# Linear-memory attention with a gated feed-forward block: transposed memory keys for two batches, and softmax denominators on VectorE for six

## The chip, the cores and the metric

The kernel runs on one NeuronCore of a Trainium2 chip. A core has five engines with queues of their own: TensorE (PE in the profile, its weight loads PEld), VectorE (DVE), ScalarE (ACT), GpSimd (POOL) and SyncE (SP), which here only issues DMAs. The metric is the device time of one execution in microseconds (us). Times vary a little from run to run, so a kernel is given by the median of several executions. One more execution is recorded by the profiler, and every duration of a single instruction comes from that one.

## The reference

There are 8 batches with 8 heads, 576 positions (S), head width 64 (D) and 32 memory slots (M). Per batch and head:

```python
a = softmax(phi, axis=positions)           # S x 32: each memory slot's weights over the positions
k_m, v_m = a.T @ k, a.T @ v                # 32 x 64 each: the memory's keys and values
attn = softmax(q @ k_m.T / 8, axis=memory) # S x 32: each position's weights over the slots
x = attn @ v_m                             # S x 64
```

The heads of a position are put side by side to a row of 512, and a feed-forward block with a gate follows, for 4608 rows:

```python
out = (silu(x @ w_gate) * (x @ w_val)) @ w_out   # 512 -> 1536 -> 512
```

## The kernel before

**Layout of the memory work.** The load of phi, k and v puts a pair of heads on 128 partitions: 64 partitions for each head, nine positions on each. So a matmul over 64 partitions and nine accumulation steps sums over the positions of one head. The kernel never forms x. Since x = attn @ v_m, it multiplies the memory's values with the gate and value weights first (`u_round`, tiles U), and then U with the attention (`gv_half`): that is one step over 128 partitions per group of four heads, 2 groups (g) per batch. A group's 128 partitions are 4 heads x 32 slots.

**Memory keys and values.** `kv_denominators` sums the phi exponentials over the positions with matmuls against a column of ones, one sum S for each head and slot; `kv_reciprocal` makes their reciprocals rS. In batches 2 to 7, `kv_items` sums keys and values together, scales both by rS on VectorE (`k_norm`, `v_norm`) and turns them with TensorE's transposes (`kv_T`) into kT, a tile of three 128-column blocks: the keys of group 0 and of group 1, and the values. In batches 0 and 1 the exponentials lie in a masked layout (`phi_exp_masked`, with zeros in the other head's rows). There the keys go the way of `k_items`: denominators, sums, `k_norm`, `kv_T`. The values are made by `v_direct`, which takes v as the stationary operand and the masked exponentials as the moving one, so that the product comes out transposed; four VectorE copies (L349) put it into kT, unscaled, and U is scaled by rS when it is evacuated (L457, L461).

**Attention.** q is transposed on TensorE for batches 0 and 1 (`q_T`) and by a transposing DMA for the others (`load_qT`). `scores(b, g)` makes 8 matmuls of a group into two banks (r, halves of the positions) and ScalarE takes the exponentials E with the factor 1/8 (L394). `z_inv(b, g)` makes the denominators: two matmuls with `bones`, a matrix with ones in 32x32 blocks on its diagonal (L405), give each column's sum over a head's 32 slots on all its partitions; two logarithms (L408) and one exponential of the negative (L410) on ScalarE give the reciprocal lz. `norm(b, g)` multiplies E by lz on VectorE into A (L415).

**Feed-forward.** A batch has 24 slots. `gv_slot` makes a gate product (two matmuls of 288 columns), silu on ScalarE (L494), and, one slot later, the value product and the multiplication on VectorE into h (L501). The output projection (L538) runs in tiles of 128 rows with 12 units of one 512-column matmul each; a full tile is copied to SBUF on VectorE ("v", L550) or ScalarE ("a", L548) and stored from SP.

**What sets the order.** Every engine's order is the order of the calls, written out by hand (`manual_schedule`). PSUM's 8 banks come from a list, oldest release first (`bank`, `done`). From batch 2 on, each batch begins with output units of the batch before (`take(n)` issues n of them), among which the scores, the value-weight round `u_values`, denominators and normalisation are placed; then the 24 slots follow, with the rest of the output units, the next batch's memory work and its U spread among them (`spread`). `phi_sum` on GpSimd adds the next batch's exponentials and waits for a batch's A (L213). Before batch 2 there is no output work to put between the steps: `warm(n)` issues dummy matmuls there (n units of 128 columns). `exp_tables()` and `preload_act_table_set` switch ScalarE's function table.

**Loads.** Inputs are loaded by GpSimd in one queue in the order of the calls: keys and q of batches 0 and 1, their values, the weights of the gate and value projections (two half blocks of block 0 for each, then blocks 1 and 2, L141), then the output weights mixed with the inputs of batches 2 and 3.

Of the kernel before, what the change touches and what calls it, by code (L numbers as in the profile page):

```python
# [9 lines left out]
FP32 = mybir.dt.float32  # L10
BF16 = mybir.dt.bfloat16
# [3 lines left out]
def kernel(  # L15
# [19 lines left out]
    nc = tc.nc  # L35
# [4 lines left out]
    M = phi.shape[3]  # L40
# [4 lines left out]
    NP = H // 2  # L45
    NJF = DF // 128
    HALF = S // 2
    CH = 512
    NCH = DF // CH
    sm_scale = 1.0 / math.sqrt(D)  # L50
# [22 lines left out]
    def bank(shape, dtype, name):  # L73
        tag = free.pop(0)
        t = ps.tile(shape, dtype, tag=tag, name=name)
        held[id(t)] = tag, t
        return t

    def done(*tiles):

        for t in tiles:
            free.append(held.pop(id(t))[0])
# [142 lines left out]
    def kv_sum(b, p, parts):  # L225


        w0, w1 = parts[0], parts[-1] + 1
        n = (w1 - w0) * D
        for j in range(JK):  # L230
            for i in range(NP):
                for g in range(NG):
                    nc.tensor.matmul(  # L233
                        p[g][32 * i:32 * i + 32, 0:n],
                        lhsT=phi_of(b, g, j, i),
                        rhs=kvs[b][64 * g:64 * g + 64, w0:w1, i, j * D:(j + 1) * D],
                        start=(j == 0),
                        stop=(j == JK - 1),
                        tile_position=(64 * g, 32 * i),
                    )  # L240
# [71 lines left out]

        return [run_sums, lambda: kv_T(b, (0, 1))]

    def k_items(b):


        def denominators():
            p = bank([128, NG], FP32, "p_S")
            kv_denominators(b, p)  # L320
            kv_reciprocal(b, p)
            done(p)

        def sums():
            p = [bank([128, D], FP32, f"p_kv{g}") for g in range(NG)]
            kv_sum(b, p, (0,))
            k_norm(b, p)
            done(*p)

        return [denominators, sums, lambda: kv_T(b, (0,))]  # L330

    def v_direct(b):

        p = bank([128, NP // 2, NG, M], FP32, "p_vT")
        for n in range(NP // 2):
            for j in range(JK):
                for o in range(2):
                    nc.tensor.matmul(
                        p[64 * o:64 * o + 64, n],
                        lhsT=kvs[b][:, 1, 2 * n + o, j * D:(j + 1) * D],  # L340
                        rhs=masked[b][:, j, :, 2 * n + o],
                        start=(j == 0),
                        stop=(j == JK - 1),
                        tile_position=(0, 64 * o),
                    )
        dst = kTs[b][:, 2].rearrange("p (n o m) -> p n o m", n=NP // 2, o=2)
        for g in range(NG):
            for o in range(2):
                nc.vector.tensor_copy(  # L349
                    out=dst[64 * g:64 * g + 64, :, o], in_=p[64 * o:64 * o + 64, :, g]  # L350
                )
        done(p)
        scaled.add(b)

# [25 lines left out]
    def scores(b, g):  # L380
        p = gv_banks()
        for i in range(NP):
            for r in range(2):
                nc.tensor.matmul(  # L384
                    p[r][32 * i:32 * i + 32, 0:HALF],
                    lhsT=kTs[b][64 * r:64 * r + 64, g, 32 * i:32 * i + 32],
                    rhs=qTs[b, i][64 * r:64 * r + 64, g],
                    start=True,
                    stop=True,
                    tile_position=(64 * r, 32 * i),  # L390
                )
        e = att.tile([128, 2, HALF], BF16, tag=f"E{g}", name="t_E")
        for r in range(2):
            nc.scalar.activation(out=e[:, r], in_=p[r][:, 0:HALF], func=AF.Exp, scale=sm_scale)  # L394
        done(*p)
        es[b, g] = e

# [2 lines left out]
    def z_inv(b, g):  # L400

        p = gv_banks()
        lz = att.tile([128, 2, HALF], FP32, tag="lz", name="t_lz")
        for r in range(2):
            nc.tensor.matmul(  # L405
                p[r][:, 0:HALF], lhsT=bones, rhs=es[b, g][:, r], start=True, stop=True
            )
            nc.scalar.activation(out=lz[:, r], in_=p[r][:, 0:HALF], func=AF.Ln)  # L408
        done(*p)
        nc.scalar.activation(out=lz, in_=lz, func=AF.Exp, scale=-1.0)  # L410
        lzs[b, g] = lz

    def norm(b, g):
# [178 lines left out]
    def out_list(b):  # L592
        tiles = range(0, 4) if b % 2 == 0 else range(4, 9)
        res = []
        for n, u in enumerate(tiles):
            if b + 1 == B and u == tiles[-1]:
                res += out_units_end(b // 2, u)
            else:
                res += out_units(b // 2, u, "v" if n % 4 != 3 else "a")
        return res  # L600

    def q_items(b, evac):
# [15 lines left out]

    def u_values(b):

        u_round(b, (((1,), 1, (0, 1)),), "vv")
    def run(items):
        for x in items:
            x()
# [13 lines left out]
    def gv_slots(b):  # L638
        return [lambda s=s: gv_slot(b, s) for s in range(2 * NJF)]

    def warm(n):


        p = bank([128, DM], FP32, "p_warm")
        x = bones.rearrange("p (a c) -> p a c", a=1)
        sizes = [4] * (n // 4)
        sizes += [n - sum(sizes)] if n > sum(sizes) else []
        for a in sizes:
            nc.tensor.matmul(  # L649
                p[:, 0:128 * a],  # L650
                lhsT=bones,
                rhs=x.to_broadcast([128, a, 128]) if a > 1 else bones,
                start=True,
                stop=True,
            )
        free.insert(0, held.pop(id(p))[0])
# [40 lines left out]


    warm(104)
    k0, k1 = k_items(0), k_items(1)  # L700
    q0, q1 = q_items(0, "vvvv"), q_items(1, "vvvv")
    run(k0[:2])
    warm(8)
    run(k0[2:] + k1[:1])
    warm(10)
    run(q0[:2])
    warm(3)
    scores(0, 0)
    run(q0[2:])
    warm(2)  # L710
    z_inv(0, 0)
    scores(0, 1)
    warm(3)
    run(k1[1:2])
    z_inv(0, 1)
    warm(2)
    run(k1[2:] + q1[:2])
    warm(4)
    scores(1, 0)
    norm(0, 0)  # L720
    run(q1[2:])
    norm(0, 1)
    warm(2)
    scores(1, 1)
    z_inv(1, 0)
    z_inv(1, 1)
    v_direct(0)
    nc.scalar.preload_act_table_set("silu_and_others")
    norm(1, 0)
    norm(1, 1)  # L730
    warm(24)
    v_direct(1)
    warm(4)


    g0, g1 = gv_slots(0), gv_slots(1)
    run([u_half(0, (0,), 0, 0, "av"), u_half(1, (0,), 0, 0, "av")])
    warm(6)
    for s in range(4):
        gv_gate(0, s)  # L740
    run([u_half(0, (1,), 0, 0, "va"), u_half(1, (1,), 0, 0, "va")])
# [20 lines left out]
    for b in range(2, B):  # L762
        last = b + 1 == B
        exp_tables()
        if b == 2:
            load_qT(2)
            phi_exp(2)
            run(take(28))
            run(kv_items(2)[:1] + take(6) + kv_items(2)[1:] + take(14))
        run(take(4))  # L770
        u_values(b)
        for g in range(NG):
            scores(b, g)
        if b == 2:
            load_k(3)
            load_v(3)
            load_q(4)
            load_phi(4, nc.gpsimd)
        run(take(6))
        if not last:  # L780
            phi_exp(b + 1)
        z_inv(b, 0)
        run(take(1))
        z_inv(b, 1)
        nc.scalar.preload_act_table_set("silu_and_others")
        run(take(13))
        norm(b, 0)
        norm(b, 1)
        if b == 2:
            run(take(4))  # L790
            u_three(2)
        run(take(12))
        g = gv_slots(b)
        beside = 0 if last else 7
        outs = [lambda: run(take(1)) for _ in range(len(backlog) - beside)]
        streams = [(g, 0, 24), (outs, 0, 24)]
        if last:
            streams += [([u_item(b, 2)], 5, 6)]
        if b == 2:
            streams += [  # L800
                ([lambda: load_qT(3)], 12, 12),
                (kv_items(3, lambda: (u_item(2, 2)(), run(take(2)))), 10, 14),
                ([lambda: (run(take(2)), u_three(3), run(take(3)))], 17, 18),
            ]
        elif not last:
            load_qT(b + 1)
        if not last:
            if b > 2:
                phi_sum(b + 1)
            if b + 3 < B:  # L810
                load_q(b + 3)
            if b + 2 < B:
                load_k(b + 2)
                load_v(b + 2)
            if b + 3 < B:
                load_phi(b + 3, nc.gpsimd)
        if not last and b > 2:
            streams += [
                (kv_items(b + 1, lambda: (u_item(b, 2)(), run(take(2)))), 9, 14),
                ([lambda: (run(take(2)), u_three(b + 1), run(take(3)))], 17, 18),  # L820
            ]
        spread(*streams)
        flush_mul()
        backlog += out_list(b)
# [29 lines left out]
```

The softmax here doesn't subtract the row's maximum and nothing guards it: scores larger than these inputs give would overflow.

## Time and profile before

| what | value |
|---|---|
| median of 9 executions | 247.6 us (246.9 to 248.25) |
| the profiled execution | 248.25 us, span 246.5 us |
| TensorE busy | 238.9 us, 97% |
| VectorE busy | 163.0 us, 66% |
| ScalarE busy | 164.0 us, 67% |
| GpSimd busy | 47.5 us, 19% |
| first gate product of batch 0 | at 28.53 us |
| output units before batch 2 start | at 56.14 us |
| scores of batches 3, 4, 5, 6, 7 | about 98.5, 124.2, 152.5, 178.4, 206.8 us |

The span is the time from the first to the last event that the profile shows; the execution's time has some 1.75 us more around it. In the timeline a line gives start, duration, engine, source line, operation, tiles (written<-read), shapes and how many instructions were merged; in brackets stands idle time and what ended it. Matmuls are pipelined: a single one of 288 columns shows 286 ns, though the next begins 122 ns after it.

### The profile page before, as it was taken

How to read it: one execution, taken by the hardware profiler on the slowest of the kernel's cores; microseconds unless marked ns; L12 is line 12 of the kernel's file. 1: busy time of each engine (PE TensorE's matmuls, PEld its weight loads, DVE VectorE, ACT ScalarE, POOL GpSimd, SP SyncE). 2: the span in 40 equal slices, each digit the busy share in tenths (PEclk: the TensorE clock that was granted, in tenths of full speed). 3: DMA queues.
4: the chain of work that ended last, by engine and by line, in shares of the span. 5: the costliest groups of instructions: out<-in, count | busy, mean ns of one | idle time of the engine just before them, and what ended most of it. 6: DMA issues, size and time to landing. Idle time of an engine off the chain costs nothing.

```text
span 246.5 us, 6654 instructions
## 1 busy us (share of the span) xinstructions
PE 238.9 (97%) x2614; PEld 142.3 (58%) x2614; DVE 163.0 (66%) x364; ACT 164.0 (67%) x350; POOL 47.5 (19%) x77
## 2 busy tenths in 40 slices
PE   7989999999999999999999999999999999999993
PEld 2454567774544755467645665476546655567543
DVE  4136799993437688479847788479746886587420
ACT  2746889885086568966896677866995668676201
POOL 8522532000320004050505410080005000000000
PEclk9999999999999999999999999999999999999999
DMA  6999999995999974997796699289416311310143
GB/s 212 206 205 204 201 208 207 254 250 94 177 212 247 233 90 73 209 303 122 115 236 216 95 199 253 67 159 165 88 45 109 78 43 45 85 43 4 43 127 85
DMA packets 42447, 37.00 MB, mean 150 GB/s; under 512 B 15920, under 2 KB 37168, under 8 KB 42416
## 3 DMA queue, kind: packets, MB, share of 16 engines
q0 software_dynamic: 21424, 22.42, 52.1%
q1 hardware_dynamic: 20240, 13.37, 23.3%
q10 hardware_dynamic: 752, 0.79, 1.0%
q8 instruction: 20, 0.33, 0.5%
q14 instruction: 11, 0.09, 0.1%
HBM read 42.47 MB, written 9.44 MB: 211 GB/s over the span
## 4 chain that ended last, share of the span: by engine, by line
PE 93%; DVE 3%; ACT 1%; DMA 1%; issue 1%
PE p_oo L538 38%; PE p_g L478 20%; PE p_v L478 19%; PE p_u L435 5%; PE p_warm L649 4%; PE p_kv L233 2%; PE p_g L384 1%; DVE t_qT L374 1%; PE p_g L405 1%; DMA out_dram<-t_o 1%; PE p_v L405 1%; DVE t_kT L349 1%; DVE t_A L415 1%; PE p_T L293 1%; ACT t_E L394 0%
## 5 line engine op out<-in xcount | busy, mean ns | idle before, releaser
L538 PE MATMUL p_oo<-WO,t_h 128*128 128x512 bf16 x420 | 108.6, 379 | 0.0
L494 ACT ACTIVATE t_sg<-p_g 128x288 bf16<-128x288 f32 x192 | 76.3, 413 | 34.0 <-PE p_g L478 27.1
L501 DVE TENSOR_TENSOR t_h<-t_sg,p_v 128x288 bf16<-128x288 bf16 x192 | 82.4, 452 | 17.3 <-PE p_v L478 13.5
L478 PEld LDWEIGHTS <-t_U 128*128 128x128 bf16 x768 | 73.9, 98 | 31.7 <-issue 2.7
L478 PE MATMUL p_g<-t_A,t_U 128*128 128x288 bf16 x384 | 77.5, 286 | 0.1
L478 PE MATMUL p_v<-t_A,t_U 128*128 128x288 bf16 x384 | 76.9, 286 | 0.0
L538 PEld LDWEIGHTS <-t_h 128*128 128x128 bf16 x420 | 39.6, 98 | 40.9 <-issue 5.9
L550 DVE COPY t_o<-p_oo 128x512 f32<-128x512 f32 x27 | 18.6, 690 | 31.4 <-PE p_oo L538 31.3
L459 DVE CAST t_U<-p_u 128x512 bf16<-128x512 f32 x42 | 26.7, 684 | 6.8 <-PE p_u L435 6.8
L455 ACT CAST t_U<-p_u 128x512 bf16<-128x512 f32 x30 | 15.8, 592 | 7.6 <-PE p_u L435 7.6
L548 ACT COPY t_o<-p_oo 128x512 f32<-128x512 f32 x8 | 4.7, 588 | 20.1 <-PE p_oo L538 20.0
L114 POOL DMA_DIRECT2D t_q<-in_q_dram x6 | 4.8, 802 | 63.2 <-DMA t_qT<-t_q 61.7
L435 PE MATMUL p_u<-W,t_kT 64*32 64x512 bf16 (+1 forms) x416 | 16.0, 365 | 0.3 <-DVE t_kT L349 0.2
L649 PE MATMUL p_warm<-bones 128*128 128x512 bf16 (+2 forms) x46 | 14.0, 437 | 1.7 <-DVE bones L672 1.7
L394 ACT ACTIVATE t_E<-p_g 128x288 bf16<-128x288 f32 x16 | 6.6, 412 | 7.6 <-PE p_v L384 7.1
L213 POOL COPY t_mark<-t_A 1x1 bf16<-1x1 bf16 x4 | 0.7, 180 | 56.2 <-DVE t_A L415 56.2
L415 DVE TENSOR_TENSOR t_A<-t_E,t_lz 128x576 bf16<-128x576 bf16 x16 | 11.4, 750 | 0.0
L410 ACT ACTIVATE t_lz<-t_lz 128x576 f32<-128x576 f32 x16 | 10.9, 683 | 0.5
L636 ACT ACT_TABLE_LOAD x7 | 9.0, 1283 | 1.4 <-PEq L838 1.3
L461 DVE TENSOR_SCALAR t_U<-p_u,t_rS 128x512 bf16<-128x512 f32 (+1 forms) x14 | 8.8, 669 | 1.4 <-PE p_u L435 1.4
L435 PEld LDWEIGHTS <-t_kT 64*32 64x32 bf16 x416 | 4.9, 89 | 8.2 <-issue 6.7
L457 ACT ACTIVATE t_U<-p_u,t_rS 128x512 bf16<-128x512 f32 (+1 forms) x14 | 8.1, 627 | 1.6 <-PE p_u L435 1.5
(66 smaller groups left out, 167.9 us busy)
## 6 DMA issues: line engine op xcount, KB each, us to landing
t_kv<-in_k_dram POOLq DMA_DIRECT2D x8, 576.0 KB, 9.2
t_kv<-in_v_dram POOLq DMA_DIRECT2D x8, 576.0 KB, 13.8
out_dram<-t_o SPq DMA_DIRECT2D x23, 192.0 KB, 2.6
t_phi<-in_phi_dram POOLq DMA_DIRECT2D x6, 576.0 KB, 16.2
t_q<-in_q_dram POOLq DMA_DIRECT2D x6, 576.0 KB, 6.8
out_dram<-t_o SPq DMA_DIRECT2D x24, 128.0 KB, 2.4
WO<-in_moe_w_out_dram POOLq DMA_DIRECT2D x3, 512.0 KB, 19.2
out_dram<-t_o SPq DMA_DIRECT2D x23, 64.0 KB, 2.1
```

Of the source, the lines that this page charges most:

```text
L410: nc.scalar.activation(out=lz, in_=lz, func=AF.Exp, scale=-1.0)
L415: nc.vector.tensor_tensor(out=a, in0=es.pop((b, g)), in1=lzs.pop((b, g)), op=ALU.mult)
L435: nc.tensor.matmul(p[g][32 * i:32 * i + 32, o:o + n], lhsT=kTs[b][64 * g:64 * g + 64, 2, 32 * i:32 * i + 32], rhs=w_part(w, c, i, g, halve ...
L455: nc.scalar.copy(out=t, in_=p)
L459: nc.vector.tensor_copy(out=t, in_=p)
L478: nc.tensor.matmul(p[:, 0:HALF], lhsT=Us[b, c, g][:, o // 2, which, 128 * (o % 2):128 * (o % 2 + 1)], rhs=atts[b, g][:, r], start=(g == 0) ...
L494: nc.scalar.activation(out=sg, in_=gate[:, 0:HALF], func=AF.Silu)
L501: nc.vector.tensor_tensor(out=dst, in0=sg, in1=val[:, 0:HALF], op=ALU.mult)
L538: nc.tensor.matmul(mine["p"], lhsT=hts[c, jf][:, 128 * u:128 * (u + 1)], rhs=WO[jf], start=(jf == 0), stop=(jf == NJF - 1),)
L550: nc.vector.tensor_copy(out=t_o, in_=mine["p"])
L636: nc.scalar.preload_act_table_set("natural_log_exp_and_others")
L649: nc.tensor.matmul(p[:, 0:128 * a], lhsT=bones, rhs=x.to_broadcast([128, a, 128]) if a > 1 else bones, start=True, stop=True,)
```

## The change

Batches 0 and 1: the memory keys are formed transposed like the values. A function `direct(b, which)` holds the product of `v_direct` for keys (0) or values (1). `k_items` now has two steps: denominators, and a direct product with four VectorE copies into kT. The keys are not scaled by rS any more; `denominators` also makes rk = rS/8, and the exponentials of the scores take their factor from rk per partition. The order of the attention of both batches is redone: the keys of batch 1 follow after the scores of batch 0, `z_inv(1, 0)` comes ahead of `scores(1, 1)`, and `v_direct(0)` ahead of `z_inv(1, 1)`; the numbers of dummy matmuls change.

Batches 2 to 7: `z_inv` is replaced by `z_inv_v`. VectorE sums E over 32x32 blocks that it transposes while reading (18 sums per partition), takes the reciprocal, and writes lz by a transpose of the broadcast reciprocals. `u_values` comes behind the scores and its two evacuations go to ScalarE. Normalisation follows each group's denominators at once, with 20 output units issued behind both. Of the output tiles of a batch the first two go to ScalarE and the others to VectorE; before, the fourth went to ScalarE. lz has three buffers.

```diff
+    def direct(b, which):
+        p = bank([128, NP // 2, NG, M], FP32, "p_mT")
+        for n in range(NP // 2):
+            for j in range(JK):
+                for o in range(2):
+                    nc.tensor.matmul(
+                        p[64 * o:64 * o + 64, n],
+                        lhsT=kvs[b][:, which, 2 * n + o, j * D:(j + 1) * D],
+                        rhs=masked[b][:, j, :, 2 * n + o],
...
+            rks[b] = att.tile([128, NG], FP32, tag="rk", name="t_rk")
+            nc.vector.tensor_scalar(
+                out=rks[b], in0=rSs[b], scalar1=sm_scale, scalar2=None, op0=ALU.mult
+            )
         def sums():
-            p = [bank([128, D], FP32, f"p_kv{g}") for g in range(NG)]
-            kv_sum(b, p, (0,))
-            k_norm(b, p)
-            done(*p)
-        return [denominators, sums, lambda: kv_T(b, (0,))]
+            p = direct(b, 0)
+            kTs[b] = att.tile([128, 3, 128], BF16, tag="kT", name="t_kT")
+            dst = kTs[b][:, 0:NG].rearrange("p g (n o m) -> p n g o m", n=NP // 2, o=2)
+            for x, e in enumerate(engs):
+                o, r = x // 2, x % 2
+                copy(e, dst[64 * r:64 * r + 64, :, :, o], p[64 * o:64 * o + 64])
+            done(p)
+        return [denominators, sums]
...
-            nc.scalar.activation(out=e[:, r], in_=p[r][:, 0:HALF], func=AF.Exp, scale=sm_scale)
+            scale = rks[b][:, g:g + 1] if b in rks else sm_scale
+            nc.scalar.activation(out=e[:, r], in_=p[r][:, 0:HALF], func=AF.Exp, scale=scale)
...
+    def z_inv_v(b, g):
+        z = att.tile([128, 2, 2 * NBL], FP32, tag="z", name="t_z")
+        nc.vector.tensor_reduce(
+            out=z[:, 0],
+            in_=es[b, g].rearrange("p r (n t) -> p (r n) t", t=32),
+            axis=mybir.AxisListType.X,
+            op=ALU.add,
+            apply_transpose=True,
+        )
+        nc.vector.reciprocal(out=z[:, 1], in_=z[:, 0])
+        lz = att.tile([128, 2, HALF], FP32, tag="lz", bufs=3, name="t_lz")
+        nc.vector.transpose(
+            out=lz.rearrange("p r (n t) -> p (r n) t", t=32),
+            in_=z[:, 1].rearrange("p (n t) -> p n t", t=1).to_broadcast([128, 2 * NBL, 32]),
+        )
...
-                res += out_units(b // 2, u, "v" if n % 4 != 3 else "a")
+                res += out_units(b // 2, u, "a" if n < 2 else "v")
...
-        u_round(b, (((1,), 1, (0, 1)),), "vv")
+        u_round(b, (((1,), 1, (0, 1)),), "aa")
...
-    run(k0[:2])
+    run(k0)
     warm(8)
-    run(k0[2:] + k1[:1])
-    warm(10)
+    run(k1[:1])
+    warm(4)
     run(q0[:2])
-    warm(3)
+    warm(2)
     scores(0, 0)
     run(q0[2:])
     warm(2)
     z_inv(0, 0)
     scores(0, 1)
+    warm(6)
+    run(k1[1:])
     warm(3)
-    run(k1[1:2])
     z_inv(0, 1)
+    run(q1[:2])
     warm(2)
-    run(k1[2:] + q1[:2])
-    warm(4)
     scores(1, 0)
     norm(0, 0)
     run(q1[2:])
     norm(0, 1)
-    warm(2)
+    warm(3)
+    z_inv(1, 0)
     scores(1, 1)
-    z_inv(1, 0)
+    warm(6)
+    v_direct(0, "vvvv")
     z_inv(1, 1)
-    v_direct(0)
     nc.scalar.preload_act_table_set("silu_and_others")
     norm(1, 0)
     norm(1, 1)
-    warm(24)
-    v_direct(1)
+    warm(16)
+    v_direct(1, "vvvv")
     warm(4)
...
-    warm(6)
     for s in range(4):
         gv_gate(0, s)
...
-        u_values(b)
         for g in range(NG):
             scores(b, g)
+        u_values(b)
...
-        run(take(6))
         if not last:
             phi_exp(b + 1)
-        z_inv(b, 0)
-        run(take(1))
-        z_inv(b, 1)
         nc.scalar.preload_act_table_set("silu_and_others")
-        run(take(13))
-        norm(b, 0)
-        norm(b, 1)
+        for g in range(NG):
+            z_inv_v(b, g)
+            norm(b, g)
+        run(take(20))
```

More of the change, by code (lines that the diff above doesn't have):

```diff
@@ L47 @@
     HALF = S // 2
+    NBL = HALF // 32
     CH = 512
@@ L313, in kv_items, with copy, k_items @@
         return [run_sums, lambda: kv_T(b, (0, 1))]
-    def k_items(b):
+    def direct(b, which):
[7 more added lines that the diff above has]
+                        rhs=masked[b][:, j, :, 2 * n + o],
+                        start=(j == 0),
+                        stop=(j == JK - 1),
+                        tile_position=(0, 64 * o),
+                    )
+        return p
+    def copy(eng, out, in_):
+        if eng == "a":
+            nc.scalar.copy(out=out, in_=in_)
+        else:
+            nc.vector.tensor_copy(out=out, in_=in_)
+    rks = {}
+    def k_items(b, engs):
         def denominators():
@@ L322, in denominators, with v_direct @@
             done(p)
+            rks[b] = att.tile([128, NG], FP32, tag="rk", name="t_rk")
+            nc.vector.tensor_scalar(
+                out=rks[b], in0=rSs[b], scalar1=sm_scale, scalar2=None, op0=ALU.mult
+            )
         def sums():
-            p = [bank([128, D], FP32, f"p_kv{g}") for g in range(NG)]
-            kv_sum(b, p, (0,))
-            k_norm(b, p)
-            done(*p)
-        return [denominators, sums, lambda: kv_T(b, (0,))]
[L332 to L345, printed above, removed]
-        dst = kTs[b][:, 2].rearrange("p (n o m) -> p n o m", n=NP // 2, o=2)
[L347 to L351, printed above, removed]
+            p = direct(b, 0)
[6 more added lines that the diff above has]
+        return [denominators, sums]
+    def v_direct(b, engs):
+        p = direct(b, 1)
+        dst = kTs[b][:, 2].rearrange("p (n o m) -> p n o m", n=NP // 2, o=2)
+        for x, e in enumerate(engs):
+            g, o = x % 2, x // 2
+            copy(e, dst[64 * g:64 * g + 64, :, o], p[64 * o:64 * o + 64, :, g])
         done(p)
@@ L402, in z_inv @@
         p = gv_banks()
-        lz = att.tile([128, 2, HALF], FP32, tag="lz", name="t_lz")
+        lz = att.tile([128, 2, HALF], FP32, tag="lz", bufs=3, name="t_lz")
         for r in range(2):
@@ L410, in z_inv @@
         nc.scalar.activation(out=lz, in_=lz, func=AF.Exp, scale=-1.0)
+        lzs[b, g] = lz
+    def z_inv_v(b, g):
[8 more added lines that the diff above has]
+        nc.vector.reciprocal(out=z[:, 1], in_=z[:, 0])
+        lz = att.tile([128, 2, HALF], FP32, tag="lz", bufs=3, name="t_lz")
+        nc.vector.transpose(
+            out=lz.rearrange("p r (n t) -> p (r n) t", t=32),
+            in_=z[:, 1].rearrange("p (n t) -> p n t", t=1).to_broadcast([128, 2 * NBL, 32]),
+        )
         lzs[b, g] = lz
@@ L639, in gv_slots, with warm @@
         return [lambda s=s: gv_slot(b, s) for s in range(2 * NJF)]
-    def warm(n):
+    def warm(n, narrow=0):
         p = bank([128, DM], FP32, "p_warm")
         x = bones.rearrange("p (a c) -> p a c", a=1)
-        sizes = [4] * (n // 4)
+        sizes = [1] * narrow + [4] * ((n - narrow) // 4)
         sizes += [n - sum(sizes)] if n > sum(sizes) else []
@@ L699 @@
     warm(104)
-    k0, k1 = k_items(0), k_items(1)
+    k0, k1 = k_items(0, "vvvv"), k_items(1, "vvvv")
     q0, q1 = q_items(0, "vvvv"), q_items(1, "vvvv")
-    run(k0[:2])
+    run(k0)
     warm(8)
-    run(k0[2:] + k1[:1])
-    warm(10)
+    run(k1[:1])
+    warm(4)
     run(q0[:2])
-    warm(3)
+    warm(2)
     scores(0, 0)
```

## The prediction

> **What bounds the kernel now.** I first read the page's first part (busy time by engine) and the fourth (the chain that ended last):
>
> ```profile
> PE 238.9 (97%) x2614; PEld 142.3 (58%) x2614; DVE 163.0 (66%) x364; ACT 164.0 (67%) x350; POOL 47.5 (19%) x77
> ...
> PE 93%; DVE 3%; ACT 1%; DMA 1%; issue 1%
> ```
>
> TensorE is busy 97% of the span and carries 93% of the chain. The clock row shows nine tenths or more in every slice, so a matmul taken from this queue should shorten the run, as long as nothing new makes TensorE wait. To see the queue I read the timeline of TensorE at the start of batch 6, which stands for batches 3 to 7:
>
> ```profile
> 178.20 0.41 PE L435 MATMUL p_u<-W,t_kT 64*32 64x512 bf16 x8
> ...
> 180.09 0.29 PE L405 MATMUL p_g<-t_E,bones 128*128 128x288 bf16 x1
> 180.21 0.29 PE L405 MATMUL p_v<-t_E,bones 128*128 128x288 bf16 x1
> 180.33 0.38 PE L538 MATMUL p_oo<-WO,t_h 128*128 128x512 bf16 x1
> 180.55 0.29 PE L405 MATMUL p_g<-t_E,bones 128*128 128x288 bf16 x1
> 180.67 0.29 PE L405 MATMUL p_v<-t_E,bones 128*128 128x288 bf16 x1
> 180.79 5.56 PE L538 MATMUL p_oo<-WO,t_h 128*128 128x512 bf16 x25
> 186.19 0.41 PE L478 MATMUL p_g<-t_A,t_U 128*128 128x288 bf16 x2
> ```
>
> The first column is the start. From start to start, a denominator matmul (L405) occupies 0.12 us, one of the output projection (L538) about 0.216 us (25 in 5.40). There is no gap. ScalarE and VectorE in the same stretch, and the table of two windows (the slots of batch 5, then this attention stretch; columns: PE, PEld, DVE, ACT, POOL busy):
>
> ```profile
> 178.79 0.41 ACT L394 ACTIVATE t_E<-p_g 128x288 bf16<-128x288 f32 x1
> 179.10 0.41 ACT L394 ACTIVATE t_E<-p_v 128x288 bf16<-128x288 f32 x1
> ...
> 183.80 1.28 ACT L785 ACT_TABLE_LOAD   x1
> ```
>
> ```profile
> 160.60:178.20 17.60, 17.60 (x232) 11.91 (x229) 15.26 (x36) 13.36 (x31) 4.73 (x8) 1.00 0.78 133
> 178.20:186.20 8.00, 8.00 (x62) 3.80 (x62) 4.00 (x6) 6.73 (x13) 0.31 (x2) 1.00 0.27 69
> ```
>
> VectorE is half idle in the attention stretch (4.00 of 8.00 us) and nearly full in the slots (15.26 of 17.60). The start differs: until 28.5 us TensorE waits for short chains through VectorE and ScalarE and fills the holes with dummy matmuls. What comes after depends on weights. TensorE and POOL's queue, both from the timeline:
>
> ```profile
> 28.53 1.14 PE L478 MATMUL p_g<-t_A,t_U 128*128 128x288 bf16 x8
> ...
> 31.42 0.63 PE L435 MATMUL p_u<-W,t_kT 64*32 64x256 bf16 x32
> ...
> 36.19 0.62 PE L435 MATMUL p_u<-W,t_kT 64*32 64x512 bf16 x16
> ```
>
> ```profile
> 25.99 0.74 POOL L156 DMA_DIRECT2D WO<-in_moe_w_out_dram  x1 [0.63 <-DMA W<-in_moe_w_gate_dram]
> ...
> 30.50 0.75 POOL L92 DMA_DIRECT2D t_phi<-in_phi_dram  x1 [1.13 <-ACT t_sg L494]
> ...
> 35.12 0.74 POOL L101 DMA_DIRECT2D t_kv<-in_v_dram  x1 [1.78 <-DMA W<-in_moe_w_val_dram]
> ```
>
> POOL issues each load when an earlier one has landed. Taken in order of issue, the first half block of gate weights is there at about 25.99, the fourth half block (value weights) at about 30.4 (I read the wait before 30.50 as this one, though the profile names ScalarE), the second value block at about 35.0. TensorE uses them at 26.70, 31.49 and 36.26: only 0.7 to 1.2 us of room.
>
> [...] the normalisation (L415) measures 750[...] the 256-column evacuation with such a scale takes 473 ns, the 288-column exponential without it 413.
>
> **Part A, denominators of batches 2 to 7.** Removed from TensorE: four L405 matmuls per batch, 2 x 0.24 us = 0.48; six batches give 2.9 us. Removed from ScalarE: four logarithms at a pace of 0.30 to 0.45 and two exponentials of 0.68, about 2.8 us per batch. Added to ScalarE: two value-weight evacuations ("vv" becomes "aa"), about 1.1, and one more output copy of 0.59. ScalarE ends with less. Added to VectorE per group: reduction 0.75[...], reciprocal of 18 columns 0.30 (2 columns take 0.171[...]; between 0.17 and 0.35), block transpose 0.78[...], then the old normalisation 0.75. With 0.04 us for each dependent step (the kv reciprocal at 63.44 lasts 0.17, its reader starts at 63.65) this is 2.75, two groups 5.5 us.
>
> Is it hidden? Scores now start at 178.20 instead of 178.42, since the value weights go behind them. The first exponential is held by the table load that ends at 178.71; both halves of group 0 are ready at about 179.43. VectorE, whose earlier products end at 178.1, is free, and finishes at 179.47 + 5.5 = 184.95. TensorE meanwhile runs scores 0.36, value weights 0.22 and 32 output matmuls 6.90, and reaches the first gate at 185.7. Cover: 0.7 us. In batch 2 four more output matmuls and 24 for U add 1.6 us. If VectorE is late the gate waits, and all slots behind it on TensorE. The output copies of that stretch leave VectorE's way: tiles 0 and 1 go to ScalarE, which gets to them at 183.5 after its table load; with eight banks in order of release the tile that waits blocks no allocation before 186. Tile 2 goes to VectorE at 185.7, after the normalisations. POOL's partial sums wait for A and start a little earlier. No DMA moves past another here, and stores follow their copies; the transposing load is later on SP and has about three microseconds before its scores.
>
> In the slots one output copy (0.69) moves from ScalarE to VectorE: 15.26 becomes 15.95 of 17.60. I cost it at nothing; the cover is VectorE's idle time of 2.3 us and the free banks for values. Without it TensorE would wait up to 0.2 to 0.4 us per batch.
>
> **Part B, the start.** The memory keys: k_sum (0.76), two scaled copies (0.61), transposes and copy (0.90 with waits) become one direct product of 36 matmuls (0.71 to 0.76 by L338) and four copies. L349's 64x64 copy takes 0.222, 64 columns more add 0.067: 4 x 0.31 = 1.23, ready at 12.89 against 12.86 before. So the keys gain nothing themselves, but TensorE loses two transposes and runs the next denominators and q transposes at once. The qT copies then start behind the keys' copies and two small scalings at 13.26 instead of 14.03: 0.77 us. For batch 1 the sums no longer go through a transpose between z and q: its first scores come at 18.98 instead of 20.22. After that v of batches 0 and 1 (21.77 and 24.62 by POOL's waits) sets some steps, and the scale pointers cost 0.1 to 0.2 per group; I get the last copies of v at 26.8 and the first gate at 27.2, 1.3 us earlier, with six dummies gone. The weights then take a part back: the fourth half block at 30.4 allows TensorE only 1.0 to 1.1 of the 31.49. I count 1.0 (bounds: 0, if a chain step is slower than I think; 1.6, if the weights are not in the way). Loads are issued at the pace at which earlier ones land, so they don't come sooner. The qT of batch 2 lands at about 65.4, its scores come at 69.1 - 1.0: still covered.
>
> **Part C, the end.** The chain's last pieces are
>
> ```profile
> 240.06 0.59 ACT t_o L548
> ...
> 240.68 2.02 DMA out_dram<-t_o
> ```
>
> The last whole tile is now copied on VectorE, 0.69 for 0.59: 0.1 us lost.
>
> Sum: -2.9 - 1.0 + 0.1 = -3.8 us. The profiled execution took 248.25 (span 246.5 and 1.75 around it) and would take 244.45. It is the highest of nine; from their median, 247.6, I get 243.8.
>
> **Rivals.**
> - Start gains nothing, part A holds: -2.8, 244.8. For it: the start's many short waits, each of which I estimate. Against: 1.3 us is found where 1.0 can be used.
> - Slots: VectorE falls behind by the added copy and TensorE waits 0.2 us in each of six batches: 243.8 + 1.2 = 245.0. Against it speaks that many products wait about 0.25 us for TensorE now.
> - [...] +1.2 us per batch, of which 0.7 is covered; 0.5 to 0.6 in five batches, some 2.8 in all: 246.6.[...]
> - Both do: +2.4, stall 1.7 in five batches and little in batch 2, 8.6 to 9: about 252.6, slower than before. The gate (L478) is the place; it decides once VectorE's two groups take 5.5 + 0.7 + 0.76 = 7.0 us.
> - That the change doesn't take the matmuls out can't be: the loop calls only the VectorE form.
>
> **How the numbers follow.** The forecast case 0.56 (243.0 to 244.6), no gain at the start 0.18, slots 0.07, one slow operation 0.10, both 0.09. The range 242.7 to 247.2 holds the first four. About 0.2% (0.5 us) is what this measurement can tell from no change. Faster by more than that: 0.56 + 0.18 + 0.07 and half of the fourth, 0.86; within: 0.04; slower: 0.10.
>
> **What would show it.** L405 with 8 instead of 32 matmuls; reduction and transpose at 0.7 to 0.85 us each; the first gate of batches 3 to 7 starting without idle time behind the output matmuls; periods of a batch shorter by 0.48; the first gate of batch 0 near 27.2 and a short wait of TensorE for weights near 30. Idle time of TensorE ahead of L478 at the first slot, named after the normalisation, would prove me wrong, as would a first gate later than 28.5.

## The result and the profile after

| | before | after |
|---|---|---|
| median | 247.46 us (32 executions) | 244.81 us (10 executions, 244.07 to 247.06) |
| ratio to before | | 0.9903, 95% interval 0.9886 to 0.9919 |
| profiled execution, its span | 248.25, 246.5 | 244.44, 242.7 |
| second comparison | 247.59 | 244.34; ratio 0.9874 (0.9852 to 0.9896) |

The change makes the kernel 2.4 to 3.2 us faster; 3.8 was forecast. Both medians lie in the range of the prediction (242.7 to 247.2), and the second also in the band of its main case (243.0 to 244.6). The first, 244.81, is what its rival without a gain at the start had (244.8), so the parts have to be measured alone. Between the two profiled executions the difference is 3.8, and how this comes about is part of what follows.

The page of the kernel after: the engines' busy time, the chain that ended last by engine, and the groups of the two new operations (line, engine, operation, written<-read, shapes, count | busy us in all, mean ns | idle time before and its releaser).

```profile
PE 234.5 (97%) x2511; PEld 139.4 (57%) x2511; DVE 172.2 (71%) x384; ACT 160.6 (66%) x334; POOL 47.5 (20%) x77
...
PE 83%; DMA 9%; DVE 3%; ACT 2%; issue 1%; POOL 1%; POOLq 0%; DVEq 0%
...
L437 DVE TRANSPOSE_TENSOR_REDUCE t_z<-t_E 128x18 f32<-128x576 bf16 x12 | 9.3, 774 | 6.1 <-ACT t_E L414 6.1
...
L446 DVE STREAM_TRANSPOSE t_lz<-t_z 128x576 f32<-128x576 f32 x12 | 9.3, 778 | 0.4
```

TensorE is still busy 97% of a span that is 3.8 us shorter. The new operations take 774 and 778 ns. What is new in the second line is DMA with 9%, where before had 1%: a transfer has come onto the chain. It does not cost 9%: the chain runs through the whole length of the transfer, and TensorE waits only for its end (0.25 us, below).

The timeline of TensorE after, at the start of batch 6, and then that of VectorE in the same stretch (start, duration):

```profile
175.61 0.40 PE L474 MATMUL p_u<-W,t_kT 64*32 64x512 bf16 x8
175.94 7.08 PE L577 MATMUL p_oo<-WO,t_h 128*128 128x512 bf16 x32
182.85 0.41 PE L517 MATMUL p_g<-t_A,t_U 128*128 128x288 bf16 x2
```

```profile
176.57 0.78 DVE L437 TRANSPOSE_TENSOR_REDUCE t_z<-t_E 128x18 f32<-128x576 bf16 x1 [1.20 <-ACT t_E L414]
177.38 0.27 DVE L444 RECIPROCAL t_z<-t_z 128x18 f32<-128x18 f32 x1
177.68 0.78 DVE L446 STREAM_TRANSPOSE t_lz<-t_z 128x576 f32<-128x576 f32 x1
178.50 0.76 DVE L454 TENSOR_TENSOR t_A<-t_E,t_lz 128x576 bf16<-128x576 bf16 x1
...
181.16 0.76 DVE L454 TENSOR_TENSOR t_A<-t_E,t_lz 128x576 bf16<-128x576 bf16 x1
```

The denominator matmuls are gone, and the first gate follows the 32 output matmuls with no idle time. VectorE's two groups take from 176.57 to 181.92, 5.35 us, and end 0.9 us before the gate. In the table of two windows (attention stretch of batch 6; columns as before: PE, PEld, DVE, ACT, POOL) VectorE has 5.38 of 8.00 us, for 4.00 before:

```profile
175.20:183.20 8.00, 8.00 (x61) 3.70 (x60) 5.38 (x10) 6.31 (x11) 1.22 (x2) 1.00 0.22 58
```

A ledger of the two profiled executions, from the starts of the same work on TensorE:

| stretch | before | after | difference |
|---|---|---|---|
| start, to the first output unit | 56.14 | 54.57 | -1.57 |
| to the scores of batch 2 | 12.94 | 12.60 | -0.34 |
| scores of batch 2 to those of batch 3 | 29.61 | 29.78 | +0.17 |
| batches 3, 4, 6: the same | 25.72, 28.30, 28.30 | 25.23, 27.81, 27.81 | -0.49 each |
| batch 5 | 25.71 | 25.36 | -0.35 |
| scores of batch 7 to the last half tile (L570; now L609) | 33.15 | 32.88 | -0.27 |
| last half tile to the end of the span | 6.63 | 6.66 | +0.03 |

The sum is -3.8. Of the second and the sixth line 0.22 each is only order: the scores now come ahead of the value weights. So every batch from 3 on gains its 0.48 but for 0.1 in batch 5, and there the 25.71 of before is the odd number (B alone and before with fewer dummies, below, take 25.83 and 25.79). Batch 2 loses 0.17 where it should gain 0.48: 0.65 us are lost there. The chain that ended last, and TensorE's timeline, say where:

```profile
59.96 6.55 DMA t_qT<-t_q
...
67.11 0.77 POOL t_q L115
67.88 0.64 POOL t_kv L98
...
68.63 14.80 DMA t_kv<-in_v_dram
...
83.47 0.86 PE p_kv L234 x72
```

```profile
83.47 0.80 PE L234 MATMUL p_kv<-t_kv,t_ephi 64*32 64x128 bf16 x72 [0.25 <-DMA t_kv<-in_v_dram]
...
86.76 0.41 PE L517 MATMUL p_g<-t_A,t_U 128*128 128x288 bf16 x2
87.36 0.40 PE L517 MATMUL p_v<-t_A,t_U 128*128 128x288 bf16 x2 [0.19 <-DVE t_o L589]
```

The first is the arrival of v of batch 3: its load stands on GpSimd behind the loads of q and k of batch 3, and that q waits until the transposing load of batch 2 has emptied its buffer (landed at 66.51, q issued at 67.11). Now v(3) is issued at 68.63 and used at 83.47, after a wait of 0.25. In the kernel before it was issued earlier, and its sums came later and without a wait (GpSimd, then TensorE):

```profile
66.90 0.77 POOL L101 DMA_DIRECT2D t_kv<-in_v_dram  x1
...
85.33 0.80 PE L233 MATMUL p_kv<-t_kv,t_ephi 64*32 64x128 bf16 x72
```

The second thing to see is a pair of value matmuls that comes 0.60 us after the gate pair instead of 0.24, held by an output copy on VectorE.

### The profile page after: what moved, and what is told of

It reads as the page before. It is cut to its first block, busy times and chain, and to the rows that moved or that the text cites. A ratio compares the mean times of both kernels' runs of the same rounds, so it can differ in the third digit from the quotient of the medians.

```text
span 242.7 us, 6458 instructions
## 1 busy us (share of the span) xinstructions
PE 234.5 (97%) x2511; PEld 139.4 (57%) x2511; DVE 172.2 (71%) x384; ACT 160.6 (66%) x334; POOL 47.5 (20%) x77
## 4 chain that ended last, share of the span: by engine, by line
PE 83%; DMA 9%; DVE 3%; ACT 2%; issue 1%; POOL 1%; POOLq 0%; DVEq 0%
PE p_oo L577 31%; PE p_v L517 18%; PE p_g L517 18%; DMA t_kv<-in_v_dram 6%; PE p_u L474 5%; PE p_warm L688 4%; DMA t_qT<-t_q 3%; PE p_kv L234 2%; PE p_oo L609 1%; PE p_g L403 1%; DVE t_qT L393 1%; PE p_q L380 1%; DVE t_kT L336 1%; ACT t_lz L428 1%; PE p_mT L322 1%
## 5 line engine op out<-in xcount | busy, mean ns | idle before, releaser
L577 PE MATMUL p_oo<-WO,t_h 128*128 128x512 bf16 x420 | 106.7, 379 | 0.0
L494 ACT CAST t_U<-p_u 128x512 bf16<-128x512 f32 x42 | 22.5, 603 | 8.3 <-PE p_u L474 8.3
L589 DVE COPY t_o<-p_oo 128x512 f32<-128x512 f32 x19 | 13.1, 688 | 17.6 <-PE p_oo L577 13.0
L498 DVE CAST t_U<-p_u 128x512 bf16<-128x512 f32 x30 | 19.0, 683 | 1.5 <-PE p_u L474 1.5
L115 POOL DMA_DIRECT2D t_q<-in_q_dram x6 | 4.8, 802 | 63.7 <-DMA t_qT<-t_q 62.2
L688 PE MATMUL p_warm<-bones 128*128 128x512 bf16 (+2 forms) x43 | 13.0, 430 | 1.7 <-DVE bones L711 1.7
L587 ACT COPY t_o<-p_oo 128x512 f32<-128x512 f32 x16 | 8.9, 587 | 7.4 <-PE p_oo L577 7.3
L437 DVE TRANSPOSE_TENSOR_REDUCE t_z<-t_E 128x18 f32<-128x576 bf16 x12 | 9.3, 774 | 6.1 <-ACT t_E L414 6.1
L454 DVE TENSOR_TENSOR t_A<-t_E,t_lz 128x576 bf16<-128x576 bf16 x16 | 12.1, 757 | 0.9 <-ACT t_lz L430 0.3
L414 ACT ACTIVATE t_E<-p_g 128x288 bf16<-128x288 f32 x12 | 5.0, 414 | 7.1 <-PE p_v L403 7.0
L446 DVE STREAM_TRANSPOSE t_lz<-t_z 128x576 f32<-128x576 f32 x12 | 9.3, 778 | 0.4
```

The lines of the kernel that those rows point to most:

```text
L437: nc.vector.tensor_reduce(out=z[:, 0], in_=es[b, g].rearrange("p r (n t) -> p (r n) t", t=32), axis=mybir.AxisListType.X, op=ALU.add, appl ...
L446: nc.vector.transpose(out=lz.rearrange("p r (n t) -> p (r n) t", t=32), in_=z[:, 1].rearrange("p (n t) -> p n t", t=1).to_broadcast([128, ...
L454: nc.vector.tensor_tensor(out=a, in0=es.pop((b, g)), in1=lzs.pop((b, g)), op=ALU.mult)
L494: nc.scalar.copy(out=t, in_=p)
L498: nc.vector.tensor_copy(out=t, in_=p)
L577: nc.tensor.matmul(mine["p"], lhsT=hts[c, jf][:, 128 * u:128 * (u + 1)], rhs=WO[jf], start=(jf == 0), stop=(jf == NJF - 1),)
```

## The experiments

**The parts alone.** The changed kernel once more; the change of batches 2 to 7 alone (A: denominators on VectorE, order of scores and value weights, engines of the output copies); and the change of batches 0 and 1 alone (B), which is the changed kernel with these parts put back:

```diff
-    out_units(b // 2, u, "a" if n < 2 else "v")
+    out_units(b // 2, u, "v" if n % 4 != 3 else "a")
...
-    u_round(b, (((1,), 1, (0, 1)),), "aa")
+    u_round(b, (((1,), 1, (0, 1)),), "vv")
...
+    u_values(b)
     for g in range(NG):
         scores(b, g)
-    u_values(b)
...
-    for g in range(NG):
-        z_inv_v(b, g)
-        norm(b, g)
-    run(take(20))
+    z_inv(b, 0)
+    run(take(1))
+    z_inv(b, 1)
...
+    run(take(13))
+    norm(b, 0)
+    norm(b, 1)
```

> The changed kernel itself, beside the others on one chip. All theories: 0.990 of before, about -2.4 us, as measured the first time.

> Part A alone: denominators of batches 2 to 7 on VectorE with its loop order and evacuation choices; the start as before. My theory (VectorE's work is hidden, 24 matmuls are gone, and what was lost of the sum is lost to the loads of batch 3, which here have 1.2 us more room): -2.8 us, ratio 0.989, and no wait for v of batch 3. Rival 1 (the missing microsecond is lost because VectorE is fuller in the slots): -1.5 us, 0.994, with TensorE waiting in the slots of every batch.

> Part B alone: keys formed transposed and the new order of the start; the loop from batch 2 on as before. My theory: -1.2 us, ratio 0.995, the first gate near 26.8 us. Rival 2 (the start gains little at the median, the profiled execution was a lucky one): -0.3 us, 0.999.

Measured against 247.59: after again 244.34, A alone 244.81 (0.9896, 0.9873 to 0.9919: 2.0 to 3.1 us), B alone 246.97 (0.9977, 0.9965 to 0.999: 0.25 to 0.9 us). A does what was forecast, with no wait for v(3). B has its first gate where it was forecast (26.81) and still brings about 0.6, half of what the theory had. Added up they make 3.1 by the ratios and 3.4 by the medians; after has 2.65 and 3.25 in its two comparisons.

**Why the start brings half.** The number of dummies at the start is fixed, and the first of them run at half pace (0.43 us apart, then 0.22). The granted clock reads 1.00 all along here, so the pace is taken from these distances. The timeline of TensorE before, and that of the changed kernel run again:

```profile
1.74 8.50 PE L649 MATMUL p_warm<-bones 128*128 128x512 bf16 x26 [1.74 <-DVE bones L672]
10.30 0.59 PE L247 MATMUL p_S<-ones,t_mphi 128*128 128x1 bf16 x18
```

```profile
1.74 7.16 PE L688 MATMUL p_warm<-bones 128*128 128x512 bf16 x26 [1.74 <-DVE bones L711]
8.96 0.59 PE L248 MATMUL p_S<-ones,t_mphi 128*128 128x1 bf16 x18
```

The same 26 matmuls end 1.34 us apart, though the change touches nothing ahead of them. So a start may be late or early by chance. To see how much the start itself can give, I took 24 of the dummies out of both kernels:

```diff
-    warm(104)
+    warm(80)
```

> The kernel before, with 80 instead of 104 units in the first series of dummy matmuls, nothing else. They end between 8.9 and 10.3 us[...], and the start hangs on them. If the start is limited by when TensorE begins, and after that by the weights' arrival (theory): TensorE begins 0.6 to 1.3 us earlier, the first output unit comes at about 54.7 us instead of 55 to 56, and the kernel gains 0.5 to 0.7 us, as much as part B alone. If part B's gain is in the chains only: no more than 0.2.

> The changed kernel with 80 instead of 104 units in the first series of dummy matmuls. By the theory (weights limit the start): no gain, within 0.2 us of the changed kernel, with longer waits for v and for weights before 36 us and the first output unit again at 54.6. If the start is still limited by the chains: 0.5 to 1 us faster.

Measured against 247.71: before with fewer dummies 246.91 (0.9978, 0.9963 to 0.9993), after with fewer dummies 244.43, where the two runs of after had 244.3 and 244.8. Taking 24 dummies out of the old start brings as much as the whole new start, and out of the new start it brings nothing that shows. The profile of this last kernel doesn't tell why: its granted clock was halved from 12 to 18 us (the third slice of this row of its page), and its first output unit came at 55.11, not at the 54.6 that was expected.

```profile
PEclk9959999999999999999999999999999999999999
```

Its other executions had a mean clock of 0.996 or more (0.986 in the profiled one), so the median stands.

What limits the new start shows in the other profiles. TensorE needs the second block of value weights for a round of U, and the trace has the time at which that block has landed. The table sets the first output unit beside it (us; two of these kernels come further below):

| kernel | dummies end | block landed | first output unit | distance |
|---|---|---|---|---|
| before | 10.24 | 34.83 | 56.14 | 21.31 |
| before with fewer dummies | 8.91 | 34.65 | 54.83 | 20.18 |
| A alone (old start) | 9.23 | 34.90 | 54.85 | 19.95 |
| after | 9.83 | 34.79 | 54.57 | 19.78 |
| after again | 8.90 | 34.83 | 54.61 | 19.78 |
| B alone | 10.03 | 34.82 | 54.61 | 19.79 |
| one more transpose (start of after) | 10.34 | 35.29 | 55.07 | 19.78 |
| q(2) earlier and the tile (start of after) | 10.45 | 34.87 | 55.03 | 20.16 |

In seven of the fourteen profiles, all with the new start, the distance is 19.78 or 19.79, although the dummies end 1.5 us apart, and in none is it less. There the load is the bound. The wait itself, in after (TensorE's weight loads, waits from 30 to 54 us):

```profile
PEld L474 <- DMA W<-in_moe_w_val_dram: 0.3, 1, 0.3
```

The old start stood 1.5 us above that bound when its dummies ended late (before) and 0.2 when they ended early (A alone). So the new start gains much in a late execution and little in an early one. In the earliest ones TensorE waits for other loads too: up to 0.51 for q and 0.28 and 0.89 for v in after run again, 0.40 for gate weights in A alone.

**Is the cover of VectorE's chain real?** To the changed kernel I added transposes of the same reciprocals into a tile that nobody reads, between the transpose and the normalisation: one per batch (group 0 alone), two (one per group), and four (two per group, shown). Nothing else differs.

```diff
+        for _ in range(2):
+            ex = att.tile([128, 2, HALF], FP32, tag="ex", bufs=1, name="t_ex")
+            nc.vector.transpose(
+                out=ex.rearrange("p r (n t) -> p (r n) t", t=32),
+                in_=z[:, 1].rearrange("p (n t) -> p n t", t=1).to_broadcast([128, 2 * NBL, 32]),
+            )
```

> The changed kernel with one more block transpose (0.78 us) on VectorE ahead of the normalisation of group 0 in batches 2 to 7, into a tile that nobody reads. In the changed kernel A of group 1 is ready about 1.1 us before the first gate. If that cover is what hides VectorE: no difference to the changed kernel (within 0.3 us). If VectorE's load itself costs time (fuller engine, later products), about 0.78 us for each of six batches would show as well in part: +1 to +4 us.

> The same with one more block transpose in each group: 1.6 us more per batch. By the cover of 1.1 us TensorE waits some 0.5 us ahead of the first gate in batches 3 to 7, not in batch 2: +2.5 us to the changed kernel. By a load cost: more than twice what the run with one more shows. By a cover that reaches further than I think: no difference.

> The changed kernel with two more block transposes in each group of batches 2 to 7. Two in all added only 1.1 us (about 0.66 each where the next does not depend on it, less what the dependence of the normalisation no longer costs) and used up the cover to within 0.1 us. Four add some 2.4 us: A comes 1.2 to 1.4 us after TensorE has reached the first gate. By the cover (theory): TensorE waits 1.2 to 1.4 us in batches 3 to 7 and nothing in batch 2, which has 1.6 us more: +6 to +7 us to the changed kernel, about 250.5 to 251.5, slower than the kernel before. If the wait is taken back later: less than +3.

One: 244.54 (0.9882). Two: 244.44 (0.987), no loss; the theory's 2.5 us more were wrong, because two more transposes make the chain only 0.94 longer (6.29 for 5.35). In this kernel's trace the extra one starts 0.70 after the transpose ahead of it, and the normalisation, which doesn't depend on the extra one, 0.66 after that: 1.36 from the transpose to the normalisation, where without the extra one it takes 0.81 to 0.88. The chain then ends at 183.00 and the first gate starts at 182.99: the cover is used up. Four: 252.3 (1.0188, 1.0162 to 1.0213), some 8 us above after run again, for 6 to 7 expected. TensorE's timeline at batch 6 of this kernel, and its waits by line (us in total, times, longest):

```profile
187.86 0.29 PE L523 MATMUL p_g<-t_A,t_U 128*128 128x288 bf16 x1
189.55 0.28 PE L523 MATMUL p_g<-t_A,t_U 128*128 128x288 bf16 x1 [1.40 <-DVE t_A L460]
```

```profile
PE p_g L523 <- DVE t_A L460: 7.0, 5, 1.4
```

The chain takes from 181.58 to 189.50, 7.9 us, and TensorE waits 1.40 at the first slot of five batches. This is the forecast's slower rival made real: its place holds, and nearly its price (8.6 to 9 were worked out, for a wait of 1.7). The extra 1.2 us per batch for a slow operation, on which that price rests, was an assumption; no trace shows one: the reduction took 774 ns and the transpose 778. The rival's threshold of 7.0 us was too high: there is no wait at 6.29, and 7.9 less the wait of 1.40 is 6.5. The cover, not idle VectorE as such, is what made A free.

**The late v.** If v(3) is late because k and v stand behind q(3), then issuing q(3) behind them should bring the loss back:

```diff
     load_q(2)
-    load_q(3)
...
             load_v(3)
+            load_q(3)
```

> The changed kernel, with the load of q of batch 3 issued behind k and v of batch 3, so that these no longer queue behind the transposing load of batch 2 on GpSimd's queue. My theory: k and v land by about 70 us, TensorE doesn't wait for v before the sums of batch 3, and 0.5 to 1.4 us of the gain come back: 0.985 to 0.988 of before. Rivals 1 and 2: no difference to the changed kernel, 0.990.

Measured: 246.42 (0.9949, 0.9931 to 0.9967), 2 us slower than after. The timelines of SP and of TensorE of this kernel:

```profile
60.17 5.94 SPq L121 DMA_TRANSPOSE t_qT<-t_q  x1
```

```profile
69.68 0.28 PE L403 MATMUL p_g<-t_qT,t_kT 64*32 64x288 bf16 x1 [2.29 <-DMA t_qT<-t_q]
```

The loads of k and v went out at 43.13 and 45.71, and the transposing load of batch 2 beside or behind them took 5.94 to issue (3.10 in after) and 9.37 to land, so that the scores of batch 2 waited 2.29. The sum for v was then on time, but at 85.66, with TensorE 2.2 us later than in after, so this doesn't test the diagnosis: the remedy moved the wait to a worse place. So next I moved what releases the queue, the load of q(2) and with it the transposing load; and, in a second kernel, I moved an output copy of batch 1 to ScalarE against the stretched pair; and both.

```diff
     load_phi(2, nc.gpsimd)
+    load_q(2)
     load_wo(2)
...
-    load_q(2)
     load_q(3)
```

```diff
-    "a" if n < 2 else "v"
+    "a" if n < 2 or (b == 1 and n == 4) else "v"
```

> The changed kernel, with q of batch 2 loaded three places earlier (ahead of the last output weights). Theory (k and v of batch 3 queue behind q of batch 3, and that behind the transposing load of batch 2): the transposing load runs earlier, v of batch 3 lands before it is needed, the wait of 0.2 to 0.3 us ahead of the sums of batch 3 goes: -0.2 us. If the transposing load slows down among the other loads by more than it starts earlier, or the output weights come too late for the first output units: no gain or up to 1 us lost.

> The changed kernel, with the fifth output tile of batch 1 copied on ScalarE instead of VectorE. It is the copy behind which the values' products of batch 2 wait at 87 us (TensorE's pair of gate matmuls there takes 0.60 instead of 0.24). Theory (VectorE is late there, a bank comes free late): 0.2 to 0.3 us less. If the pair is late for another reason: no difference.

> Both of these edits: the sum of what each gives, -0.4 to -0.5 us to the changed kernel by the theory, about 0.985 of before.

Measured against 247.73: q(2) earlier 244.26 (0.986, 0.9835 to 0.9885), the tile 244.57 (0.9868), both 244.21 (0.986). With q(2) earlier the transposing load starts at 53.55, q, k and v of batch 3 go out at 62.60 to 64.13, and the sum at 83.28, as early as in after, has no wait: here the diagnosis is shown. From the scores of batch 2 to those of batch 3 it takes 29.46 (29.78 in after). That gain of 0.3 lies within what these medians can tell apart: the two kernels with q(2) earlier have the lowest medians, but are not shown to be faster than after. The tile did nothing, and its profile shows why: the copies of batch 1's first three tiles run at 72.20 (two, ScalarE) and 75.75, so the copy that holds the pair, at 86.63, is the fourth (n = 3), and I had moved the fifth. Moving the fourth was not tried.

Without that run, the parts alone still say which part the stretched pair belongs to. VectorE after, and ScalarE of B alone:

```profile
85.43 1.28 DVE L498 CAST t_U<-p_u 128x512 bf16<-128x512 f32 x2
86.63 0.68 DVE L589 COPY t_o<-p_oo 128x512 f32<-128x512 f32 x1
87.22 0.81 DVE L540 TENSOR_TENSOR t_h<-t_sg,p_v 128x288 bf16<-128x288 bf16 x2
```

```profile
85.70 0.61 ACT L587 COPY t_o<-p_oo 128x512 f32<-128x512 f32 x1
```

In every profile with part A the copy stands on VectorE behind the scaling of keys and values and two U casts, the products wait behind it, and TensorE shows the wait of 0.19 (0.20 in one). In B alone and before, the copy is on ScalarE and there is no such wait. The time from batch 2 to batch 3 agrees: 29.61 in before and in B alone, 29.47 in A alone where 29.13 was due: 0.34 lost.

## Why the prediction was right or wrong

**Part A, right in mechanism and size.** Four matmuls fewer per batch gave 0.49 in batches 3, 4 and 6, for 0.48. VectorE's prices were 0.75, 0.30, 0.78 and 0.75; measured 0.774, 0.266, 0.778 and 0.757. The first three were the author's estimates, which no trace of before shows; the fourth had been measured there (750 ns). The transposing reduction and the transpose come out close to the normalisation of as many columns: 774 and 778 ns against 757. For the reciprocal the estimate added 0.13 us to the 171 ns of two columns; 18 columns took 266 ns, so the 16 further ones took 95 ns, some 6 ns each. The two groups took 5.35 us for 5.5, and that is most of why the cover was 0.9 for 0.7. One step of the part failed: for the added output copy on VectorE the prediction said "I cost it at nothing". It was free in five batches; in batch 2 it cost 0.34 (by A alone; no run moved that copy), where it falls in behind the next batch's keys and values. That is the slots rival in one batch out of six. VectorE's average idle time in the slots (2.3 us) said nothing about that moment.

**Part B, wrong in size.** The sum had 1.0; alone it brings 0.57 by the ratio. The working of the chain was sound in the main: keys ready at 12.42 (12.89 forecast, and all of the start was 0.41 earlier with its dummies; a copy took 222 ns with 64 columns and 288 with 128, and the keys' four took 1.21 us for 1.23) and the first gate at 26.75 (27.2; it is 27.23 where the dummies end at 10.45). One link was longer: the scores of batch 1 came at 18.99 (18.98), 0.4 late against that shift, and TensorE waits 0.34 for qT there. The limit by the weights was misread. The prediction took a wait of GpSimd before 30.50, which the profile puts down to ScalarE, for the fourth half block, and so cut 1.3 us to 1.0. By the trace this block landed at 29.94 before and 29.67 after, and TensorE's round with it starts at 29.69 without a wait. The block that binds is the second one of the value weights, which left 1.5 us; TensorE waits 0.25 for it at 34.8. So the profiled execution gained more than forecast. What failed for the median is the last step, "I count 1.0", as a gain of every execution: it starts from one execution, whose dummies ended late, and whose first output unit at 56.14 no other profile of this study repeats. With the dummies early, as in A alone, the old start reaches 54.85, and little is left to gain. The scale pointer on the exponentials, for which the prediction counted 0.1 to 0.2 us per group, costs 78 ns on each of a group's two (491 ns in after against 413 in before), 0.16 per group.

**The step to the median, wrong.** The sum of -3.8 gives 244.45 for the profiled execution, and 244.44 was measured. That looks exact and is partly luck: the start gave 1.57 and not 1.0, and batch 2 lost 0.65. Carrying the whole difference to the median took the late start of this one execution along. The text said that it was the highest of nine and did not ask what made it so.

**A queue that was not followed, wrong.** "The qT of batch 2 lands at about 65.4" was checked against its own scores and stopped there. Behind it on GpSimd stand q, k and v of batch 3. The transposing load did not move with TensorE: it starts at 59.92 before and 59.96 after. That alone would have cost nothing: in A alone v(3) is issued at 67.00, TensorE comes to the sums at 83.43, as early as in after, and doesn't wait. But in after the load also landed later, at 66.5 for 64.8. So v(3) came 1.7 us later, and TensorE waited 0.16 to 0.47 in five of the seven profiles that have both parts and these loads in the order of after.

The traces' records of DMA packets suggest why it lands later; no run tested it. The load ends with 32 writes of 4 bytes. In before they come together, at 64.04 to 64.29. In after 30 of them come at 64.10 to 64.42, and a single one at 66.44, just ahead of the landing. From 64.48 to 65.40 runs a packet of 16384 bytes of the queue that the page calls "instruction". In all eight profiles with the new start and the old order of these loads, where the load takes 6.1 to 6.6 us to land, such a packet runs between 63.7 and 65.8. In before, A alone and before with fewer dummies, where it takes 4.9 to 5.0, none runs between 58.7 and 66.1. So the new start seems to have moved one of these packets onto this load.

**The end** cost 0.03 for 0.1: the end hangs on the two half tiles, and the whole tile's copy on VectorE is not on that path.

Taken together for the medians: -2.9 (A) - 0.6 (B) + 0.34 (copy) + 0 to 0.5 (v) makes -3.2 to -2.7; 2.65 and 3.25 were measured. The difference between these two comparisons is not settled by the runs.

## What to carry to other kernels

When the bounding engine gets faster, look up every transfer whose issue hangs on something that does not move with it, and follow the queue behind it to the last load, not to the next one. A sum made against one profiled execution holds for that execution; ask what made it slow or fast before its difference is carried to the median. Where a load is suspected to be the bound, compare over several executions the distance from its landing to a fixed later point: it is constant where the load binds (here 19.78 or 19.79 in seven profiles). Work moved to an engine that is idle on average is free only if, at each place where it lands, the chain it joins ends before its consumer needs it; adding dummy work until the time moves measures that room directly.

## What was not expected of the hardware

- A reduction over 32x32 blocks that are transposed while they are read cost about as much as another pass over 576 columns: 774 ns for 128x576 bf16 to 128x18, against 757 for the normalisation.
- On VectorE an operation of 576 columns that doesn't depend on the one just before it started 0.66 to 0.70 us after that one (two more transposes), though each shows 0.72 to 0.78; a dependent one started 0.81 to 0.88 after (in after).
- TensorE came to full pace (dummies 0.43 us apart, then 0.22) between 4.3 and 7.7 us into the profile in executions with the same first matmuls; 26 dummies ended between 8.8 and 10.5. So this moment differs between executions, and a gain worked out from one of them carries it along. With the same start, dummies that ended 1.0 us later left the first output unit 1.3 us later (before against A alone).
- The transposing load of batch 2 took 3.10 us to issue in after (0 GB/s in the microsecond from 60 us), 5.94 with the loads of k and v of batch 3 sent out ahead of it, and 6.50 with q(2) earlier. In after itself the next one took 3.10 again, at 205 GB/s in its first microsecond, and the one after it 5.44, at 391 GB/s.
